# The 48 left-over gated features as 32 and 16 rows in four row groups of TensorE, instead of 48 rows in two

## The chip, the cores and the metric

The kernel runs on one core of one Trainium2 chip. The metric is the device time of one execution in microseconds (us). The engines have short names in the profile: PE is TensorE (PEld its weight loads), DVE is VectorE, ACT is ScalarE, POOL is GpSimd, SP is SyncE; SPq, ACTq and POOLq stand for what their sequencers do, DMA issues above all.

## The reference

`x` is 2048 tokens by 512 features. It is normalised, and two blocks of work are added to it.

```python
def _A_ref(x, wqkv, wo):                  # sliding local attention, 32 heads of 16
    ...
    logits = jnp.einsum('bhsd,bhswd->bhsw', q, kg) * scale     # 8 keys at distance 0, 2, ... 14
    attn = _softmax(logits, axis=-1)
    o = jnp.einsum('bhsw,bhswd->bhsd', attn, vg)
    return (lambda x, *d: x.transpose(*d))(o, 0, 2, 1, 3).reshape(B, S, D) @ wo
def _B_ref(x, w_in, w_sp, b_sp, w_out):   # gated mixer, Fh = 688
    z = _gelu(jnp.einsum('bsd,df->bsf', x, w_in))
    z1 = z[..., :Fh].copy()
    z2 = _layernorm(z[..., Fh:], axis=-1)
    g = jnp.einsum('ts,bsf->btf', w_sp, z2) + b_sp[None, :, None]
    return jnp.einsum('bsf,fd->bsd', z1 * g, w_out)
...
return x + _A_ref(xn, A_wqkv, A_wo) + _B_ref(xn, B_w_in, B_w_sp, B_b_sp, B_w_out)
```

The last step is what the change touches: for every token, a sum over 512 attention features and 688 gated features. 688 is five times 128 and 48 more.

## The kernel before, in words

The tokens are 16 tiles of 128, in two halves `th` of eight tiles. Two hand-written lists, `ten` (TensorE and ScalarE) and `vec` (VectorE), give the order of the work; `advance` interleaves them, so that each engine and each DMA queue gets its instructions in a fixed order. The stages are: layer norm and turning of `x`; the projections; the local attention on VectorE (lines 289 to 360); 16 mixing tiles `M0` to `M15` on TensorE (`mix_tile`, line 374), each with an eviction on ScalarE (line 377) that gives a gate `g`; and the output stage, lines 409 to 431 and 540 to 577.

**Gates and their turning.** `gate(j, g)` (line 382) multiplies tile `j`'s 688 features by its gate on VectorE, and SP then turns the result by DMA transposes into `uT[th]`: six blocks `m` of 128 features, features along the partitions, tokens along the free axis. Of the sixth block (`MF` = 5) 48 rows are features. For the tiles with `j // 2` even one transpose of six blocks does it (line 386), and the 48 rows land on partitions 0 to 47. For the others there are two, one of five blocks (line 388) and one of a block that begins 64 features earlier (line 389), so that the 48 rows land on partitions 64 to 111.

**The output stage.** For each tile of tokens one PSUM bank gathers three products: `gated_full` (line 413), five matmuls of 128 rows by 512 columns; `gated_rest` (line 419), one matmul of 48 rows in a row group of 64 (`tile_position=(r, 0)`, `r` 0 or 64), so that two tiles of tokens can run in TensorE side by side; and the attention, 16 matmuls of 32 rows in one of four row groups (lines 425 and 562), so that four tiles run side by side. Four tiles are a group: tiles 0, 2, 4, 6, then 1, 3, 5, 7, then 8, 10, 12, 14, then 9, 11, 13, 15. `Q0` (`out_pair`) does the first two groups in the order full, rest, rest, attention, attention, full; `Q2` (`out_group`) the third as full, rest, attention; `Q3` (`out_last`) the fourth as attention, rest, full, its last tile in two halves of 256 columns. `finish` and `finish_pair` (lines 430, 437) add `x` on VectorE and send the sum out from SP's queue.

**Loads that the steps touch.** `W0` to `W7` are SP's DMA transposes of the mixing weights (line 367). `load_wout` (lines 401, 403) loads the output weights from ACT's queue, the 48 rows twice, at partitions 0 and 64. `load_wo` (line 398) and the first half of `x` for `finish` (`X0`, line 406) are issued on ACT too, the second half (`X1`, line 406) on SP, into a buffer that `M13` frees. In `vec`, `X1` stands behind `g15`.

Of the kernel before, what the change touches and what calls it, by code (L numbers as in the profile page):

```python
# [7 lines left out]
BF16 = mybir.dt.bfloat16  # L8
# [5 lines left out]
P = 128  # L14
S = 2048
D = 512
# [8 lines left out]
HS = S // 2  # L25
GS = HS // 4
FH = 688
F = 2 * FH
FHALF = FH // 2
MF = FH // P  # L30
FREST = FH - MF * P
# [7 lines left out]
def kernel(  # L39
# [14 lines left out]
    A = nc.scalar  # L54
    G = nc.gpsimd
    PE = nc.tensor
    SP = nc.sync
# [4 lines left out]
    sb = ctx.enter_context(tc.tile_pool(name="sb", bufs=1))  # L62
# [30 lines left out]
    wout = wts[:, DH * D:(DH + MF + 1) * D].rearrange("p (m n) -> p m n", m=MF + 1)  # L93
    qk_r = [sb.tile([P, QKH], BF16, name=f"qk{t}") for t in range(2)]
    qk = [r[:].rearrange("p (a c s) -> p a c s", a=2, c=C) for r in qk_r]
    uT = [r[:, 0:(MF + 1) * HS].rearrange("p (m s) -> p m s", m=MF + 1) for r in qk_r]
    gs = [qk_r[0][:, (MF + 1) * HS + n * FH:(MF + 1) * HS + (n + 1) * FH] for n in range(3)]
    prod = [sb.tile([P, 2 * C * HS], BF16, name=f"prod{n}")[:] for n in range(2)]
    z2_r = sb.tile([P, NT * FH], BF16, name="z2")
# [281 lines left out]
    def gate(j, g):  # L381
        V.tensor_tensor(z1u[:, j, 0:FH], g, z1u[:, j, 0:FH], ALU.mult)
        th, t0 = j // 8, (j % 8) * P

        if j // 2 % 2 == 0:
            SP.dma_start_transpose(uT[th][:, :, t0:t0 + P], z1u[:, j, :])
        else:
            SP.dma_start_transpose(uT[th][:, 0:MF, t0:t0 + P], z1u[:, j, 0:MF * P])
            SP.dma_start_transpose(uT[th][:, MF, t0:t0 + P], z1u[:, j, MF * P - 64:MF * P + 64])

    def idle(n, k=1):

# [6 lines left out]

    def load_wout():  # L400
        A.dma_start(wout[:, 0:MF, :], B_w_out[0:MF * P, :].rearrange("(m p) n -> p m n", p=P))
        for r in (0, 64):
            A.dma_start(wout[r:r + FREST, MF, :], B_w_out[MF * P:FH, :])

    def load_res(th):
        (SP if th else A).dma_start(xr[th], x2[th * HS:(th + 1) * HS, :].rearrange("(i p) d -> p i d", p=P))
# [5 lines left out]
        for m in range(MF):  # L412
            PE.matmul(po[:, cols], uT[th][:, m, t0:t0 + P], wout[:, m, cols], start=(start and m == 0), stop=(stop and m == MF - 1))  # L413

    def gated_rest(tiles, start, stop, bank=None, cols=slice(0, D)):
        for i in tiles:
            r, t0 = 64 * (i // 2 % 2), (i % 8) * P
            b = po[i] if bank is None else bank
            PE.matmul(b[:, cols], uT[i // 8][r:r + FREST, MF, t0:t0 + P], wout[r:r + FREST, MF, cols],  # L419
                      start=start, stop=stop, tile_position=(r, 0))  # L420

    def attention_out(th, s, pos, start, stop):
        for d in range(DH):
# [21 lines left out]
    for i in range(5, NT):  # L445
# [4 lines left out]
        p01 p02 zs8 m10 zn8 zn9 zn10 zn11 p03 W1 f10 zs12 p10 zn12 zn13 zn14 zn15  # L450
        m11 d11 x0 m12 g0 d12 p11 u0 g1 m13 p12 W2 W3 f13 p13 c0 g2
        a0.0 a0.1 g3 x1 a0.2 a0.3 g4 a0.4 g5 a0.5 a0.6 a0.7 g6 u1 a0.8 g7 a0.9 g8 a0.10 g9 a0.11 c1 g10
        a1.0 a1.1 g11 a1.2 a1.3 g12 a1.4 g13 a1.5 g14 a1.6 a1.7 g15 X1 a1.8 a1.9 F0 a1.10 a1.11 F1 F2
    """.split()
    ten = """
        T0 T1 B GL z0 z1 h0 T3 h1 z2 h2 z3 h3 LZ k00 k01 q0 k02 q1 k03 q2 z4 q3 h4 k10 k12 k11 k13
# [75 lines left out]
    def out_pair():  # L532

        first, second = groups[0], groups[1]
        for i in first:
            gated_full(i, po[i], True, False)
        gated_rest(first, False, False)
        gated_rest(second, True, False)
        attention_out(0, 0, [po[i] for i in first], False, True)
        attention_out(0, 1, [po[i] for i in second], False, False)  # L540
        for i in second:
            gated_full(i, po[i], False, True)

    def out_group(n):
        tiles = groups[n]
        for i in tiles:
            gated_full(i, po[i], True, False)
        gated_rest(tiles, False, False)
        attention_out(n // 2, n % 2, [po[i] for i in tiles], False, True)

    def out_last(n):

        tiles = groups[n]
        th, s, last = n // 2, n % 2, tiles[-1]
        hb = [po[last], po[groups[n - 1][0]]]
        cols = [slice(0, D // 2), slice(D // 2, D)]
        for d in range(DH):
            for g in range(4):
                a = slice(32 * g, 32 * g + 32)
                for dd, b, c in [(d, po[tiles[g]], slice(0, D))] if g < 3 else \  # L560
                        [(2 * d % DH + x, hb[d // 8], cols[d // 8]) for x in range(2)]:
                    PE.matmul(b[:, c], op[a, th, dd, s * P:(s + 1) * P], wo_r[a, dd, c],  # L562
                              start=(dd == 0), stop=False, tile_position=(32 * g, 0))
        gated_rest(tiles[:3], False, False)
        for b, c in zip(hb, cols):
            gated_rest([last], False, False, b, c)
        for i in tiles[:3]:
            gated_full(i, po[i], False, True)
            finish(i, po[i])
        for b, c in zip(hb, cols):  # L570
            gated_full(last, b, False, True, c)
            finish(last, b, c)
# [4 lines left out]
    def do(n):  # L577
        k, a = n[0], n[1:]
        i = int(a) if a.isdigit() else 0
        th, w2 = (int(a[0]), int(a[1])) if len(a) == 2 and a.isdigit() else (i, 0)  # L580
        if k == "T":
            turn_pe(i)
            if i == 0:
                idle(1)
        elif n[:2] == "zs":
            z2_stats(int(n[2:]), 4)
        elif n[:2] == "zn":
            z2_norm(int(n[2:]), False)
        elif n == "z0":

            gates["z0"], gates["z1"] = nxt("mm", mm), nxt("mm", mm)
            for t, hh in ((0, 0), (1, 0), (0, 1)):
                z_half(t, 1, gates[f"z{t}"], hh)
        elif n == "z1":
            turn_pe(2)
            z_half(1, 1, gates["z1"], 1)
        elif k == "z":
            gates[n] = z_part(i, 1)
        elif k == "h":
            z2_gelu(i, gates[f"z{i}"])  # L600
        elif k == "q":
            z2_square(i)
        elif k == "k":
            qk_chunks(th, w2 // 2, w2 % 2)
        elif k == "v":
            v_pair(i)
        elif k == "H":
            v_halo()
        elif k == "S":
            head_sum(th, w2)  # L610
        elif k == "B":

            pb = mm[2][:, 1, :].bitcast(BF16)[:, 0:NT]
            PE.transpose(pb, b16[:], ident[0:NT, 0:NT])
            A.copy(b_col[:], pb)
        elif k == "y":
            z1_tile(i)
        elif k == "M":
            gates[i] = mix_tile(i)
        elif k == "W":  # L620
            load_wsp(i)
        elif k == "O":
            load_wo(i) if i < 4 else load_wout()
        elif k == "X":
            load_res(i)
        elif n == "GL":
            A.preload_act_table(ACT.Gelu_apprx_tanh)
        elif n[:2] == "EG":
            A.preload_act_table(ACT.Gelu_apprx_tanh)
        elif n[:2] == "EL":  # L630
            A.preload_act_table_set("natural_log_exp_and_others")
        elif k == "Q":
            [out_pair, None, lambda: out_group(2), lambda: out_last(3)][i]()
        elif k == "F":
            tiles = groups[i]
            for t in (0, 2):
                if (i, t) in ((0, 0), (0, 2), (1, 0)):
                    finish_pair(tiles[t])
                else:
                    finish(tiles[t], po[tiles[t]])  # L640
                    finish(tiles[t + 1], po[tiles[t + 1]])
        elif k == "e":
            softmax_exp(i)
        elif k == "i":
            softmax_inv(i)
        elif k == "s":
            ln_stats(i)
        elif k == "R":
            ln_root_act(i, 1)
        elif k == "V":  # L650
            ln_inv(i)
        elif n == "LE":
            load_early()
        elif k == "r":
            ln_root(i, 1)
        elif k == "n":
            ln_norm(i)
        elif k == "t":
            turn_dma(i)
        elif n == "LZ":  # L660
            load_x(12, 4, A)
        elif n == "LX":
            load_tokens()
        elif n == "LW":
            load_weights()
        elif k == "m":
            run(prod_ops(th, w2)[0])
        elif k == "j":
            run(prod_ops(th, w2)[1])
        elif k == "f":  # L670
            prod_ops(th, w2)[2]()
        elif k == "p":
            prod_ops(th, w2)[3]()
        elif k == "d":
            fold_dma(th, w2)
        elif k == "K":
            k_halo()
        elif k == "x":
            run(softmax_max(i))
        elif k == "u":  # L680
            run(softmax_sum(i))
        elif k == "c":
            run(softmax_scale(i))
        elif k == "g":
            gate(i, gates[i])
        elif k == "a":
            at[int(a[0])][int(a[2:])]()
        done.add(n)
# [53 lines left out]
```

## Time and profile before

| what | value |
|---|---|
| time, median of 3 runs (lowest to highest) | 202.16 us (202.12 to 202.41) |
| the profiled execution's own time | 202.3 us |
| its span in the profile | 200.6 us |
| granted TensorE clock | 0.997 |
| DVE busy | 175.7 us (88%) |
| ACT busy | 96.0 us (48%) |
| POOL busy | 38.7 us (19%) |
| read from HBM, written to it | 10.03 MB, 2.10 MB |

The span runs from the first to the last thing that the profiler saw; the execution's own time is 1.7 us longer. Busy shares are averages over stages. A busy PE means that some matmul is in the array; whether matmuls follow each other at full pace is read from their start times in the timeline, which is in order of time: start, duration, engine, line, operation, tiles, shape, count. Rows of the timeline with a count merge instructions that follow each other; the duration is then that of all of them.

### The profile page before, as it was taken

How to read it: one execution, taken by the hardware profiler on the slowest of the kernel's cores; microseconds unless marked ns; L12 is line 12 of the kernel's file. 1: busy time of each engine (PE TensorE's matmuls, PEld its weight loads, DVE VectorE, ACT ScalarE, POOL GpSimd, SP SyncE). 2: the span in 40 equal slices, each digit the busy share in tenths (PEclk: the TensorE clock that was granted, in tenths of full speed). 3: DMA queues.
4: the chain of work that ended last, by engine and by line, in shares of the span. 5: the costliest groups of instructions: out<-in, count | busy, mean ns of one | idle time of the engine just before them, and what ended most of it. 6: DMA issues, size and time to landing. Idle time of an engine off the chain costs nothing.

```text
span 200.6 us, 3841 instructions
## 1 busy us (share of the span) xinstructions
PE 195.9 (98%) x1587; PEld 118.2 (59%) x1587; DVE 175.7 (88%) x192; ACT 96.0 (48%) x149; POOL 38.7 (19%) x62
## 2 busy tenths in 40 slices
PE   7999999999999999999999999999999999999993
PEld 2645555555656666666566666666666654444652
DVE  4887879999899799999979999999999799897333
ACT  3869879998998647885533264311222110000000
POOL 4366681138660431600000000000000000000000
PEclk9999999999999999999999999999999999999998
DMA  6999459399653837999979099996949611712023
GB/s 183 288 250 197 102 117 303 106 184 206 132 110 29 184 65 146 186 101 89 248 168 192 9 259 281 156 259 128 266 82 272 135 43 39 252 65 105 5 103 105
DMA packets 64289, 30.84 MB, mean 154 GB/s; under 512 B 53440, under 2 KB 62512, under 8 KB 64144
## 3 DMA queue, kind: packets, MB, share of 16 engines
q1 hardware_dynamic: 59296, 19.23, 46.4%
q0 software_dynamic: 1904, 6.59, 16.5%
q10 hardware_dynamic: 3072, 4.78, 8.8%
q8 instruction: 12, 0.20, 0.4%
q14 instruction: 5, 0.04, 0.1%
HBM read 10.03 MB, written 2.10 MB: 60 GB/s over the span
## 4 chain that ended last, share of the span: by engine, by line
PE 88%; DMA 6%; DVE 3%; POOL 1%; issue 0%
PE mm L374 37%; PE mm L209 16%; PE mm L254 10%; PE mm L269 7%; PE mm L413 7%; PE mm L425 5%; DMA z<-in_A_x_dram 4%; DMA xnT<-z 2%; PE aux L413 2%; DVE stats L182 1%; PE mm L562 1%; PE mm L419 1%; PE aux L305 1%; DVE z L196 1%; POOL rstd L187 1%; PE aux L562 0%
## 5 line engine op out<-in xcount | busy, mean ns | idle before, releaser
L374 PE MATMUL mm<-z,wsp 128*128 128x344 bf16 x512 | 75.7, 309 | 0.0
L374 PEld LDWEIGHTS <-wsp 128*128 128x128 bf16 x512 | 50.0, 98 | 24.9 <-issue 0.4
L209 PE MATMUL mm<-wts,xnT 128*128 128x344 bf16 x256 | 40.5, 309 | 0.0
L377 ACT ACTIVATE qk<-mm,b_col 128x688 bf16<-128x688 f32 x16 | 13.3, 834 | 49.8 <-PE mm L374 49.8
L347 DVE TENSOR_TENSOR prod<-vp,a_sb 128x4096 bf16<-128x4096 bf16 x16 | 36.0, 2284 | 0.0
L209 PEld LDWEIGHTS <-xnT 128*128 128x128 bf16 x256 | 24.6, 98 | 14.0 <-issue 0.8
L254 PE MATMUL mm<-xnT,wts 128*128 128x512 bf16 x128 | 29.1, 379 | 0.3 <-DMA xnT<-z 0.2
L289 DVE TENSOR_TENSOR prod<-qk 128x4096 bf16<-128x4096 bf16 (+1 forms) x14 | 27.1, 1979 | 0.1
L351 DVE TENSOR_TENSOR prod<-prod,prod 128x8192 bf16<-128x8192 bf16 x6 | 26.5, 4420 | 0.1
L254 PEld LDWEIGHTS <-wts 128*128 128x128 bf16 x128 | 14.3, 114 | 13.1 <-issue 0.9
L256 ACT CAST qk<-mm 128x1024 bf16<-128x1024 f32 x16 | 16.2, 1011 | 4.8 <-PE mm L254 3.0
L413 PE MATMUL mm<-wts,qk 128*128 128x512 bf16 (+1 forms) x65 | 14.7, 371 | 0.0
L269 PE MATMUL mm<-xnT,wts 128*32 128x512 bf16 x256 | 14.6, 381 | 0.0
L246 ACT ACTIVATE z<-mm 128x688 bf16<-128x688 f32 x16 | 11.8, 745 | 4.5 <-PE mm L209 4.5
L182 DVE BATCH_NORM_STATS2 stats<-z 128x6 f32<-128x512 bf16 x16 | 10.9, 683 | 3.4 <-DMA z<-in_A_x_dram 3.4
L413 PEld LDWEIGHTS <-qk 128*128 128x128 bf16 x85 | 8.1, 98 | 9.2 <-issue 0.6
L220 ACT ACTIVATE z<-mm 128x688 bf16<-128x688 f32 x16 | 11.9, 744 | 1.8 <-PE mm L209 1.8
L225 ACT ACTIVATE z_junk<-z 128x688 bf16<-128x688 bf16 x16 | 12.4, 778 | 0.3
L269 PEld LDWEIGHTS <-wts 128*32 128x32 bf16 x256 | 9.3, 139 | 4.6 <-issue 0.6
L430 DVE TENSOR_TENSOR z<-mm,wsp 128x512 bf16<-128x512 f32 (+1 forms) x8 | 5.0, 653 | 8.0 <-PE mm L425 4.8
L298 POOL DMA_DIRECT2D prod<-prod x8 | 7.1, 933 | 20.9 <-DVE prod L289 19.5
L425 PE MATMUL mm<-wts,xnT 32*128 32x512 bf16 x160 | 10.7, 375 | 0.0
(93 smaller groups left out, 186.2 us busy)
## 6 DMA issues: line engine op xcount, KB each, us to landing
prod<-prod POOLq DMA_DIRECT2D x8, 512.0 KB, 5.7
wts<-in_A_wo_dram ACTq DMA_DIRECT2D x4, 512.0 KB, 5.5
out_dram<-z SPq DMA_DIRECT2D x9, 128.0 KB, 1.7
z<-in_A_x_dram SPq DMA_DIRECT2D x4, 256.0 KB, 4.4
wts<-in_A_wqkv_dram SPq DMA_DIRECT2D x2, 512.0 KB, 7.0
z<-z POOLq DMA_DIRECT2D x2, 512.0 KB, 5.6
wsp<-in_A_x_dram ACTq DMA_DIRECT2D x1, 1024.0 KB, 6.3
wsp<-in_A_x_dram SPq DMA_DIRECT2D x1, 1024.0 KB, 5.3
```

Of the source, the lines that this page charges most:

```text
L182: V.bn_stats(stats[:, i, :], xs[:, i, :])
L209: PE.matmul(pz[:, hh, 0:FHALF], xnT[:, kc, i * P:(i + 1) * P], w_z2[:, hh, kc] if part else w_z1[:, kc, hh * FHALF:(hh + 1) * FHALF], star ...
L254: PE.matmul(pq[:, cc, :], w_c[:, kc], xnT[:, kc, t0:t0 + D], start=(kc == 0), stop=(kc == C - 1))
L256: A.copy(qk[b // 2][:, a, 2 * c2:2 * c2 + 2, o:o + D], pq[:])
L269: PE.matmul(pv[32 * g:32 * g + 32, dd, :], w, r, start=(kc == 0), stop=(kc == C - 1), tile_position=(0, 32 * g))
L289: ops.append(lambda ww=ww, k=k, c=c: V.tensor_tensor(pr[:, ww, c], q[:, c], k[:, c], ALU.mult))
L347: return lambda: V.tensor_tensor(dst, vp[:, :, th, off:off + GS], a_sb[:, th, w].unsqueeze(1).broadcast_to([P, DH, GS]), ALU.mult)
L351: return lambda: V.tensor_tensor(dst, dst, x, ALU.add)
L374: PE.matmul(pg[:, hh, 0:FHALF], w[:, k, (j % 2) * P:(j % 2 + 1) * P], z2[:, k, hh * FHALF:(hh + 1) * FHALF], start=(k == 0), stop=(k == NT ...
L377: A.activation(g.rearrange("p (a b) -> p a b", a=2), pg[:, :, 0:FHALF], ACT.Identity, bias=b_col[:, j:j + 1])
L413: PE.matmul(po[:, cols], uT[th][:, m, t0:t0 + P], wout[:, m, cols], start=(start and m == 0), stop=(stop and m == MF - 1))
L425: PE.matmul(pos[g], op[32 * g:32 * g + 32, th, d, s * P:(s + 1) * P], wo_r[32 * g:32 * g + 32, d, :], start=(start and d == 0), stop=(stop ...
```

## The change

Each tile's 48 left-over features are cut into a part `x = 0` of 32 rows and a part `x = 1` of 16 rows. Tile `i` uses the row group `g` that its attention uses (`i % 8 // 2`). Every gated tile is turned by one six-block transpose, so that the 48 rows always land on partitions 0 to 47, and small SBUF-to-SBUF copies (`spread_rest`) bring the parts to the partitions of their row groups, two tiles (256 tokens) at a time. Of the eight pairs of `g` and `x`, two are in place already, so that there are six copies for each half of the tokens: those of the first half on POOL's queue behind `g7`, those of the second half on SP's queue behind `g9`, `g11`, `g13` and `g15`. Copied parts that would collide in `uT` go to a new strip `uB` in the spent query and key buffer of the second half, and their weights to a new tile `wB`. `load_wout` has eight DMAs instead of three, five on ACT and three on POOL. `X1` moves from behind `g15` to behind `g13`.

```diff
+    uB = [qk_r[1][:, (MF + 1 + n) * HS:(MF + 2 + n) * HS] for n in range(2)]
+    wB = sb.tile([P, D], BF16, name="wB")
...
     def gate(j, g):
         V.tensor_tensor(z1u[:, j, 0:FH], g, z1u[:, j, 0:FH], ALU.mult)
         th, t0 = j // 8, (j % 8) * P
-        if j // 2 % 2 == 0:
-            SP.dma_start_transpose(uT[th][:, :, t0:t0 + P], z1u[:, j, :])
-        else:
-            SP.dma_start_transpose(uT[th][:, 0:MF, t0:t0 + P], z1u[:, j, 0:MF * P])
-            SP.dma_start_transpose(uT[th][:, MF, t0:t0 + P], z1u[:, j, MF * P - 64:MF * P + 64])
+        SP.dma_start_transpose(uT[th][:, :, t0:t0 + P], z1u[:, j, :])
...
-        for r in (0, 64):
-            A.dma_start(wout[r:r + FREST, MF, :], B_w_out[MF * P:FH, :])
+        last, first = B_w_out[MF * P + 32:FH, :], B_w_out[MF * P:MF * P + 32, :]
+        A.dma_start(wout[0:FREST, MF, :], B_w_out[MF * P:FH, :])
+        A.dma_start(wout[64:96, MF, :], first)
+        G.dma_start(wout[96:P, MF, :], first)
+        G.dma_start(wB[32:64, :], first)
+        for r, q in ((0, G), (64, A), (96, A)):
+            q.dma_start(wB[r:r + FREST - 32, :], last)
...
-    def gated_rest(tiles, start, stop, bank=None, cols=slice(0, D)):
-        for i in tiles:
-            r, t0 = 64 * (i // 2 % 2), (i % 8) * P
-            b = po[i] if bank is None else bank
-            PE.matmul(b[:, cols], uT[i // 8][r:r + FREST, MF, t0:t0 + P], wout[r:r + FREST, MF, cols],
-                      start=start, stop=stop, tile_position=(r, 0))
+    def rest_of(i, x):
+        g, t0 = i % 8 // 2, i % 8 * P
+        rows = slice(32 * g, 32 * g + (FREST - 32 if x else 32))
+        if (x == 0) != (g == 1):
+            return rows, uT[i // 8][rows, MF, t0:t0 + P], wout[rows, MF]
+        return rows, uB[i // 8][rows, t0:t0 + P], wB[rows]
+    def gated_rest(tiles, start, last=None):
+        for x in range(2):
+            for i in tiles:
+                rows, u, w = rest_of(i, x)
+                for b, c in last if last and i == tiles[3] else [(po[i], slice(0, D))]:
+                    PE.matmul(b[:, c], u, w[:, c], start=(start and x == 0), stop=False, tile_position=(rows.start, 0))
+    def spread_rest(th, g):
+        t = slice(2 * g * P, 2 * (g + 1) * P)
+        for x in range(2):
+            dst = (uT[th][:, MF] if (x == 0) != (g == 1) else uB[th])
+            n, r = (FREST - 32, 32) if x else (32, 0)
+            if (g, x) not in ((0, 0), (1, 1)):
+                (SP if th else G).dma_start(dst[32 * g:32 * g + n, t], uT[th][r:r + n, MF, t])
...
-        a1.0 a1.1 g11 a1.2 a1.3 g12 a1.4 g13 a1.5 g14 a1.6 a1.7 g15 X1 a1.8 a1.9 F0 a1.10 a1.11 F1 F2
+        a1.0 a1.1 g11 a1.2 a1.3 g12 a1.4 g13 X1 a1.5 g14 a1.6 g15 a1.7 a1.8 a1.9 F0 a1.10 a1.11 F1 F2
...
-        gated_rest(tiles[:3], False, False)
-        for b, c in zip(hb, cols):
-            gated_rest([last], False, False, b, c)
+        gated_rest(tiles, False, list(zip(hb, cols)))
...
         elif k == "g":
             gate(i, gates[i])
+            if i in (7, 9, 11, 13, 15):
+                for g in range(4) if i == 7 else [(i - 9) // 2]:
+                    spread_rest(i // 8, g)
```

In `vec`, `g15` also moves ahead of `a1.7`, an addition over 128x8192 elements of the attention on VectorE (line 351).

More of the change, by code (lines that the diff above doesn't have):

```diff
@@ L536, in out_pair @@
             gated_full(i, po[i], True, False)
-        gated_rest(first, False, False)
-        gated_rest(second, True, False)
+        gated_rest(first, False)
+        gated_rest(second, True)
         attention_out(0, 0, [po[i] for i in first], False, True)
@@ L547, in out_group @@
             gated_full(i, po[i], True, False)
-        gated_rest(tiles, False, False)
+        gated_rest(tiles, False)
         attention_out(n // 2, n % 2, [po[i] for i in tiles], False, True)
```

## The prediction

> **What bounds the kernel now.** I read the page's busy rows first, then the chain that ended last, then the waits of PE, then the timeline of PE in the output stage.
>
> ```profile
> PE 195.9 (98%) x1587; PEld 118.2 (59%) x1587; DVE 175.7 (88%) x192; ACT 96.0 (48%) x149; POOL 38.7 (19%) x62
> ...
> PE   7999999999999999999999999999999999999993
> ...
> PE 88%; DMA 6%; DVE 3%; POOL 1%; issue 0%
> ```
>
> PE is in work in every slice but the first and the last, and 88% of the chain is its own. In the list of waits, PE's matmuls waited for something else for 1.3 us in the whole run, all of it before the output stage. So a nanosecond that leaves PE's stream after `M15` leaves the time, as long as nothing else becomes late, and a faster DMA or VectorE gains nothing by itself.
>
> Is PE at full pace there? In the timeline of PE around `Q0`:
>
> ```profile
> 163.62 4.48 PE L413 MATMUL mm<-wts,qk 128*128 128x512 bf16 x20
> 168.03 0.82 PE L419 MATMUL mm<-wts,qk 48*128 48x512 bf16 x5
> 168.47 0.38 PE L419 MATMUL aux<-wts,qk 48*128 48x512 bf16 x1
> 168.69 0.38 PE L419 MATMUL mm<-wts,qk 48*128 48x512 bf16 x1
> 168.69 0.38 PE L419 MATMUL aux<-wts,qk 48*128 48x512 bf16 x1
> 169.00 0.61 PE L425 MATMUL mm<-wts,xnT 32*128 32x512 bf16 x8
> ```
>
> One matmul lasts 0.379 us, but the next starts sooner: 20 full ones take 4.48 = 19 steps + 0.379, a step of 0.216. The 48-row matmuls go in pairs: eight of them fill four steps (starts at 168.03, .25, .47, .69). The attention goes in fours: 31 steps lie between its first start (169.00) and its last (175.70, in the same timeline), 0.216 each. And at every change of form there is a hole. 163.62 + 20 x 0.216 = 167.94, and the 48-row matmuls start at 168.03: 0.09. 168.03 + 4 x 0.216 = 168.89, and the attention starts at 169.00: 0.11. Attention back to full: 175.92 against 176.01, 0.09.
>
> The same in `Q2` and `Q3`:
>
> ```profile
> 184.75 0.61 PE L419 MATMUL mm<-wts,qk 48*128 48x512 bf16 x4
> 185.29 0.61 PE L425 MATMUL mm<-wts,xnT 32*128 32x512 bf16 x8
> ```
> ```profile
> 192.00 0.42 PE L562 MATMUL mm<-wts,xnT 32*128 32x512 bf16 x3
> 192.35 0.39 PE L419 MATMUL mm<-wts,qk 48*128 48x512 bf16 x1
> ...
> 192.69 0.27 PE L419 MATMUL mm<-wts,qk 48*128 48x256 bf16 x1
> 192.89 0.60 PE L413 MATMUL mm<-wts,qk 128*128 128x512 bf16 x2
> ```
>
> `Q2`: 184.75 + 0.43 = 185.18 against 185.29, a hole of 0.11. `Q3`: 192.22 against 192.35, 0.13; the 48-row part lasts 0.45 (its last half starts at 192.69 and streams 0.11), then 0.09. From 185.29 to 188.76 and on into `Q3`'s attention, also in fours, there is none: it is the change of the number of row groups that costs, not the change of stage.
>
> **The change, part by part.**
>
> *The matmuls.* 17 matmuls of 48 rows become 34 of 32 or 16 rows. They run four abreast in the attention's own row groups, so the steps stay: eight tiles in `Q0` were four pairs and are four fours, in `Q2` two and two, in `Q3` 0.45 becomes 2 x 0.216 = 0.43. Gone are the holes between rest and attention: 0.11 (`Q0`), 0.11 (`Q2`), 0.13 plus 0.02 (`Q3`). Sum -0.37 us. Two holes become full to four groups, which the trace does not show. Bounds: nothing, or the widest hole, 0.13, for each; I take 0.09, that of full to two groups, the nearest row. With the bounds the gain is 0.29 to 0.55.
>
> A rule that speaks against it: the Trainium skill (TensorE: Matmul & The Clock Gate, section "Measured speedup vs the span model") gives 3.07 times for four row tiles of 32 by 512, not four times. This trace shows four matmuls in a step of 0.216; what the rule would make here is the second rival below.
>
> *Transposes.* Eight pairs of DMA transposes on SP become single ones. An issue holds SP's sequencer for 1.2 us (median of lines 386, 388, 389), so 10 us of queue go. Nothing waited for them, so nothing is gained; `W7`, which stood behind `g6`'s second one, is issued about 1.3 us sooner.
>
> *Copies on SP.* Six copies, each set behind the landing of the transposes before it, and what is behind them in the queue waits too: `g10` to `g15`, `X1`, the stores. With 4.5 us from issue to landing (median of line 386) and 0.5 us per copy (line 406's issue), I walk the queue: `g9` issued 145.4, landed 149.9; `g11` issued 151.7, landed 156.2; `g13` issued 158.0, landed 162.5; `X1` 163.5, `g15` 165.3, landed 169.8; its two copies on their way by 170.8, landed by 175.5 with the 4.7 us of the 48-row loads (line 403). `Q2`'s rest needs them at 184.65. Cover: 9 us; cost nothing. The 1 MB of `X1` now moves beside `g14`'s and `g15`'s transposes; it landed in 5.3 us, less than the cover. The first store, at 173.98, is not held up.
>
> *Copies and loads on POOL.* Three loads and six copies. POOL has no work after 85 us. The last two copies wait for `g7` (issued about 141 us); at 1.7 us an issue and 12.4 us to land, the dearest rows of POOL's queue (line 274), they are there by 161, and the rest needs them at 168.03. Cost nothing. DVE beside POOL's issues kept its pace (line 289: 2281 to 2293 ns), so I charge DVE nothing.
>
> *ACT's queue.* Two more issues of 0.5 us (line 403) ahead of the exponential at 119.96. It ends at 122.9 instead of 121.9; DVE reads it at 124.81, and `M7`'s eviction comes at 126.48. A `wo` load behind it now waits for `W5`, issued at 113.6 and landed at 123.9 by the slowest of line 367 (10.3 us): a hold of under 1 us. Cost nothing; PE has three banks in turn.
>
> *`g15` ahead of `a1.7`.* This is the part with the thinnest cover. The timeline of DVE:
>
> ```profile
> 160.45 2.29 DVE L347 TENSOR_TENSOR prod<-vp,a_sb 128x4096 bf16<-128x4096 bf16 x1
> 162.77 4.43 DVE L351 TENSOR_TENSOR prod<-prod,prod 128x8192 bf16<-128x8192 bf16 x1
> 167.11 0.51 DVE L382 TENSOR_TENSOR z<-qk,z 128x688 bf16<-128x688 bf16 x1
> 167.54 4.49 DVE L347 TENSOR_TENSOR prod<-vp,a_sb 128x4096 bf16<-128x4096 bf16 x2
> ```
>
> Now DVE's queue stops at `g15` until `M15` is evicted (163.82 + 0.83 = 164.65, ACT's timeline), 1.9 us idle, with `a1.7` to `a1.11`, `F0` and `F1` behind it. Then 0.43 + 4.34 + 4.49 to 173.95; the 0.64 us that DVE waited for `Q0` before is used up; `F0` 2.40, `a1.10` and `a1.11` 6.66: done at 183.0 instead of 181.7. `Q2`'s attention needs it at 185.08. Cover 2.1 us (3.5 before); cost nothing. `F1` ends at 185.5, `Q3` needs its banks at 188.55; `F0` ends at 176.4, `Q2` needs its banks at 180.34.
>
> *Sum.* 202.30 (the profiled execution: span 200.6 and 1.7 around it) - 0.37 = 201.93. The median of the runs is 0.14 lower than that execution, so the forecast for a median is **201.8 us**, 0.18% less.
>
> **The rivals.**
>
> 1. *SP's copies come late* (the slower end). Mechanism: four landings in a row, each holding the queue. The point is `Q2`'s rest at 184.65. If each landing took the longest of line 386, 9.4 us, `g15` would land at 189.4, its copies at 194.1, and PE would wait 9.5 us: 211. It decides only if the four together are 9 us over the median; each us beyond costs one. For it: the landings range from 2.3 to 9.4. Against: the median is 4.5, and the DMA engines are busy for a third of 160 to 180 us. Chance 5%.
> 2. *Four row groups do not pack fully in so short a run.* If only two ran abreast, as with 64 rows, the eight steps (four in `Q0`, two each in `Q2` and `Q3`) would be sixteen: 8 x 0.216 = 1.7 more, 203.5, slower. Against: after the hole at 169.00 the eight attention matmuls go in fours from the first, 0.61 = 0.216 + 0.379 and little more. 3%. By the skill's factor it would be eight steps times 4 / 3.07 - 1, an estimate of 0.52 more: 202.3, within the bound.
> 3. *The change doesn't do what it says:* going from 32 to 16 rows, or back, opens a hole of its own. Four passes to `x = 1` and three back, 0.1 each, take back 0.7: 202.5, no change by the bound. Against: both parts are set to row groups of 32, and 48 rows in groups of 64 ran pair after pair with no hole. 6%.
> 4. *DVE late at `Q2`*, by over the 2.1 us of cover: 1 us over gives 202.8. 3%.
>
> **How the numbers follow.** The forecast has 81%; 2% are left for what I do not see. About 0.2%, 0.40 us, is what a measurement can tell from no change, so the line lies at 201.76, 0.04 below the forecast; the runs shown scatter by 0.15 about their middle. With the bounds of 0.29 to 0.55, 43 of the 81 lie beyond the line: faster 0.43. Within it lie the other 38, rival 3 and half of the unseen: 0.45. Slower are rivals 1, 2 and 4 and the other half: 0.12. The range: a gain of 0.55 and some scatter give 201.4 below, rival 3 gives 202.5 above; rivals 1, 2 and 4 and the unseen, 13%, stay outside.
>
> **What would show it.** In the changed timeline of PE the rest and the attention follow each other with no hole in `Q0`, `Q2` and `Q3`; the rest starts every 0.216 us in fours; one hole of about 0.09 stands ahead of the rest in `Q0` and `Q2`, none in `Q3`. DVE waits about 1.9 us ahead of `g15` and is through `a1.11` near 183. PE's list of waits shows no DMA and no DVE after `M15`. A hole ahead of the rest of `Q2` with a DMA as releaser is rival 1, ahead of its attention with DVE rival 4, a step over 0.216 within a rest rival 2, a hole between its halves rival 3.

## The result, and the profile after

The changed kernel takes 201.63 us (median of 7 runs, 201.42 to 201.79) against 202.12 us of the kernel before beside it (7 runs). The ratio is 0.9973, 95% interval 0.9962 to 0.9984: 0.3 to 0.8 us faster. Run again later (`e9_change_again`), it gave 0.9985 (0.9968 to 1.0002), an interval that just includes no change. Its profiled execution took 201.5 us with a span of 199.8.

The engines' busy row of the page is nearly as it was; PE still bounds the kernel:

```profile
PE 194.8 (98%) x1604; PEld 119.0 (60%) x1604; DVE 176.0 (88%) x192; ACT 95.9 (48%) x149; POOL 41.1 (21%) x71
```

PE has 17 matmuls more and is busy 1.1 us less; that sum is no measure of the gain, as the kernel before, run again, shows 194.3 (`e1_before_again`, where 8 of the 1587 matmuls have no record). The timeline of PE around `Q0` (start, duration, line, tiles, shape, count; full matmuls are now line 417, the rest 432, the attention 445 and 582):

```profile
163.22 4.48 PE L417 MATMUL mm<-wts,qk 128*128 128x512 bf16 x20
167.63 0.39 PE L432 MATMUL mm<-wts,qk 32*128 32x512 bf16 x1
...
167.86 0.38 PE L432 MATMUL mm<-wB,qk 16*128 16x512 bf16 x1
...
168.08 0.37 PE L432 MATMUL mm<-wts,qk 32*128 32x512 bf16 x1
...
168.30 0.37 PE L432 MATMUL mm<-wB,qk 16*128 16x512 bf16 x1
...
168.51 1.03 PE L445 MATMUL mm<-wts,xnT 32*128 32x512 bf16 x16
```

Four fours start at 167.63, .86, 168.08 and .30, the attention at 168.51: no hole between rest and attention, none between 32 and 16 rows. The hole ahead of the rest is 0.09 (163.22 + 20 x 0.216 = 167.54). From the rest to the attention it took 0.97 us before and takes 0.88 now. `Q2` (0.54 before, 0.45 now) and `Q3`:

```profile
184.26 0.39 PE L432 MATMUL mm<-wts,qk 32*128 32x512 bf16 x1
...
184.71 1.46 PE L445 MATMUL mm<-wts,xnT 32*128 32x512 bf16 x24
```
```profile
191.62 0.37 PE L432 MATMUL mm<-wts,qk 32*128 32x512 bf16 x1
...
191.66 0.27 PE L432 MATMUL aux<-wts,qk 32*128 32x256 bf16 x1
191.77 0.27 PE L432 MATMUL mm<-wts,qk 32*128 32x256 bf16 x1
...
191.88 0.27 PE L432 MATMUL aux<-wB,qk 16*128 16x256 bf16 x1
192.00 0.27 PE L432 MATMUL mm<-wB,qk 16*128 16x256 bf16 x1
192.19 1.25 PE L417 MATMUL mm<-wts,qk 128*128 128x512 bf16 x5
```

In `Q3` the last tile's half-matmuls are the slow strand: they start 0.04 behind the others and follow each other in 0.11 to 0.12, so that the rest takes 0.57 to the full matmuls (0.54 before), while `Q2`'s attention and `Q3`'s, with the hole behind them, shrank from 7.06 (185.29 to 192.35) to 6.91 (184.71 to 191.62). In all: 0.09 + 0.09 + 0.15 - 0.03 = 0.30 us less. From the first rest of `Q0` to the last addition on VectorE it was 29.40 us (168.03 to 197.43) and is 29.11 (167.63 to 196.74):

```profile
197.43 0.42 DVE L430 TENSOR_TENSOR z<-mm,wsp 128x256 bf16<-128x256 f32 x1
```
```profile
196.74 0.42 DVE L450 TENSOR_TENSOR z<-mm,wsp 128x256 bf16<-128x256 f32 x1
```

The first line is of before, the second of the changed kernel. This length, "the stage" below, is the same to 0.01 us in every trace of kernels with the same PE order, which makes it a finer measure than the time.

Two things are left over. The first rest starts 0.40 earlier (167.63 against 168.03), and behind the last store's landing the span ends sooner: 0.91 us against 1.03.

### The profile page after: what moved, and what is told of

Read it like the earlier page. It is cut to its first block, busy times and chain, and to the rows that moved or that the text cites. A ratio compares the mean times of both kernels' runs of the same rounds, so it can differ in the third digit from the quotient of the medians.

```text
span 199.8 us, 3885 instructions
## 1 busy us (share of the span) xinstructions
PE 194.8 (98%) x1604; PEld 119.0 (60%) x1604; DVE 176.0 (88%) x192; ACT 95.9 (48%) x149; POOL 41.1 (21%) x71
## 4 chain that ended last, share of the span: by engine, by line
PE 95%; DMA 1%; DVE 1%; SPq 0%; issue 0%
PE mm L378 37%; PE mm L213 19%; PE mm L258 14%; PE mm L273 7%; PE mm L417 7%; PE mm L445 5%; PE aux L417 2%; DMA z<-in_A_x_dram 1%; PE mm L582 1%; PE mm L432 1%; PE aux L309 1%; PE aux L205 0%; PE aux L582 0%; DVE z L200 0%; DVE stats L186 0%; DVE z L450 0%
## 5 line engine op out<-in xcount | busy, mean ns | idle before, releaser
L440 POOL DMA_DIRECT2D qk<-qk x6 | 3.0, 500 | 50.5 <-DMA wB<-in_B_w_out_dram 27.9
L386 DVE TENSOR_TENSOR z<-qk,z 128x688 bf16<-128x688 bf16 x16 | 8.2, 510 | 4.3 <-ACT qk L381 4.3
```

## The experiments

Each kernel was timed in three or five rounds against the kernel before on the same chip. "End" is from the landing of the last store (by the trace, 2.12 to 2.15 us after the last addition starts) to the end of the span. The last column but one is worked out from the trace: 1 + (stage + end - 29.40 - 1.03) / 202.

```
kernel                    first rest  stage   end   worked out  ratio to before (95%)
before                      168.03    29.40  1.03   1           -
changed                     167.63    29.11  0.91   0.9980      0.9973 (0.9962 to 0.9984)
e1_before_again             167.72    29.40  1.03   1.0000      1.0008 (0.9999 to 1.0018)
e2_wB_alone                 167.61    29.41  1.29   1.0013      1.0010 (1.0001 to 1.0019)
e3_order_alone              167.97    29.40  1.04   1.0000      1.0006 (0.9990 to 1.0022)
e4_no_copies                167.85    29.11  1.28   0.9998      0.9994 (0.9986 to 1.0003)
e5_turns_alone              167.46    29.40  1.30   1.0013      1.0014 (1.0004 to 1.0024)
e6_two_more_holes           167.74    29.32  0.91   0.9990      0.9987 (0.9977 to 0.9998)
e7_vector_late              167.71    31.64  0.92   1.0105      1.0152 (1.0125 to 1.0178)
e8_old_order                168.19    29.10  0.91   0.9979      0.9989 (0.9973 to 1.0005)
e9_change_again             167.46    29.10  0.91   0.9979      0.9985 (0.9968 to 1.0002)
e10_last_tile_first         168.16    29.11  0.92   0.9980      0.9981 (0.9965 to 0.9997)
e11_vector_late_by_half     167.66    29.51  0.91   1.0000      1.0003 (0.9983 to 1.0023)
e12_one_more_dma            167.57    29.11  1.35   1.0001      0.9995 (0.9984 to 1.0006)
```

### Is the early start part of the change?

`e1_before_again` is the kernel before, without an edit.

> The kernel before, unchanged, run once more against itself. Theory A (the gain is the holes of the output stage, 0.30 us from the first full matmul of Q0 on; the 0.40 us by which that stage began earlier in the changed kernel's trace, 163.22 against 163.62, is how the loads of x happened to land): ratio 1.000 with an interval of about 0.001 to each side, and the start of Q0 in this trace lies anywhere between 163.2 and 163.7, while the stage itself, first full matmul of Q0 to last half-matmul of Q3, again takes 33.07. Theory B (the early 0.40 belongs to the change: layout of SBUF or the new loads): Q0 starts at 163.6 again.

`e2_wB_alone`:

```diff
+    wB = sb.tile([P, D], BF16, name="wB")
...
+        G.dma_start(wB[32:64, :], first)
+        for r, q in ((0, G), (64, A), (96, A)):
+            q.dma_start(wB[r:r + FREST - 32, :], last)
```

> The kernel before with the tile wB and its four loads added (every later tile moves by 1 KB), and nothing that reads them. Theory A: no effect, ratio 0.999 to 1.001, output stage 33.07. Theory B: Q0 starts at about 163.2 and the ratio is 0.998 (0.4 us of 202).

The same program started its first rest at 168.03 and at 167.72. Over the table the old rest starts between 167.46 and 168.03 (mean 167.76), the changed one between 167.46 and 168.19 (mean 167.77). So the 0.40 is not the change. In the trace of before a tile of `x` kept VectorE waiting for 0.59 us ahead of 13.83 and PE stood at 20.20; in `e1` and in the changed kernel's trace neither shows. The traces of `e3`, `e8` and `e10` have this wait too, with 0.52 to 1.02 us, and these and before are the four with the latest start, whichever rest they have. (`e6` waits for 0.59 us as well and starts at 167.74, so the wait is not the whole of it.) `wB` does nothing to the stage. Theory B falls.

### Do the order, the transposes or the copies matter?

`e3_order_alone`, the kernel before with:

```diff
-        a1.0 a1.1 g11 a1.2 a1.3 g12 a1.4 g13 a1.5 g14 a1.6 a1.7 g15 X1 a1.8 a1.9 F0 a1.10 a1.11 F1 F2
+        a1.0 a1.1 g11 a1.2 a1.3 g12 a1.4 g13 X1 a1.5 g14 a1.6 g15 a1.7 a1.8 a1.9 F0 a1.10 a1.11 F1 F2
```

> The kernel before with the changed order only: X1 behind g13, g15 ahead of a1.7. Theory A: no effect on the time, ratio 0.999 to 1.001, stage 33.07; VectorE is idle about 1.9 us ahead of g15 and is through a1.11 about 1 us later than before (182.9 against 181.7). Theory C (the order brings part of the gain): ratio 0.998 or less, or a stage shorter than 33.0.

`e8_old_order`, the changed kernel with those two lines the other way round:

> The changed kernel with the old order of VectorE's list: g15 behind a1.7, X1 behind g15. Theory A: the order is worth nothing either way; from the first rest of Q0 to the last addition on VectorE 29.10 us, ratio to before 0.998 to 1.000, though SP sends the last copies some 2 us later. Theory F (without the new order the last copies come late): PE waits for a DMA ahead of Q2's rest and the stage is longer than 29.2.

`e5_turns_alone`, the kernel before with single transposes, as in the change, and whole 48-row copies:

```diff
...
+            if i in (7, 11, 15):
+                for g in (1, 3) if i == 7 else [(i - 9) // 2]:
+                    t = slice(2 * g * P, 2 * (g + 1) * P)
+                    u = uT[i // 8]
+                    (SP if i > 7 else G).dma_start(u[64:64 + FREST, MF, t], u[0:FREST, MF, t])
```

> One six-block transpose for every tile, as in the change, but the 48 rows stay whole, in two row groups of 64; four copies bring them to partition 64 (two on POOL's queue for the first half of the tokens, two on SP's for the second). Theory A (only the holes count; eight transposes fewer on SP gain nothing): from the first rest of Q0 to the last addition on VectorE 29.40 us, as in all four traces with the old rest (the two with the new one have 29.11), and a ratio to before of 0.9995 to 1.002, as the kernel before run against itself gave. Theory D (transposes fewer are part of the gain): 0.998 or less.

`e4_no_copies`, the changed kernel without the calls of `spread_rest` (so it leaves out what brings six of the eight parts to their places):

> The changed kernel without its twelve small copies, so that six of the eight parts of the left-over features are read from stale rows. Theory A (copies are wholly hidden): the same time as the changed kernel, ratio to before 0.997 to 0.9985, stage 32.77 as in the changed kernel. Theory D (the copies cost something on PE or DVE): faster than the changed kernel, ratio under 0.996, or a stage under 32.7.

All four keep the stage of their matmul order, 29.40 or 29.10: order, transposes and copies are hidden. One thing came out the other way than expected: in `e8_old_order` SP sent the last two copies not later but sooner, at 170.37 against 173.09, since there `X1` stands behind them in its queue. The first line is of the changed kernel, the second of `e8_old_order`:

```profile
173.09 1.18 SPq L440 DMA_DIRECT2D qk<-qk  x2
```
```profile
170.37 1.15 SPq L440 DMA_DIRECT2D qk<-qk  x2
```

And by its median `e4_no_copies` was not as fast as the changed kernel (0.9994; the interval overlaps that of `e9`), and `e5_turns_alone` was slower than before, though their stages are right. What they have in common with `e2_wB_alone` is the end, 1.28 to 1.30 instead of 0.91 or 1.03; that is taken up below.

### Is it the holes?

`e6_two_more_holes`, the changed kernel with, in `out_pair` (the new last argument marks the end of the sum in PSUM):

```diff
-        gated_rest(second, True)
         attention_out(0, 0, [po[i] for i in first], False, True)
-        attention_out(0, 1, [po[i] for i in second], False, False)
+        attention_out(0, 1, [po[i] for i in second], True, False)
         for i in second:
-            gated_full(i, po[i], False, True)
+            gated_full(i, po[i], False, False)
+        gated_rest(second, False, None, True)
```

> The changed kernel with the rest of the second group (tiles 1, 3, 5, 7) moved behind that group's full matmuls, so that PE passes once more from full rows to four row groups and back; no matmul more or less. Theory A: two holes of 0.09 more, stage 29.11 + 0.18 = 29.29 us, ratio about 0.0009 above that of the changed kernel run beside it. Theory E (the holes are not what the change saved; it is the matmuls in fours that are faster): stage 29.11.

Its timeline of PE, where the two forms now meet:

```profile
178.45 1.24 PE L417 MATMUL aux<-wts,qk 128*128 128x512 bf16 x5
179.62 0.39 PE L432 MATMUL mm<-wts,qk 32*128 32x512 bf16 x1
...
180.17 0.39 PE L417 MATMUL mm<-wts,qk 128*128 128x512 bf16 x1
```

178.45 + 5 x 0.216 = 179.53: a hole of 0.09 ahead; 179.62 + 2 x 0.22 = 180.06: 0.11 behind. The stage grew by 0.21 with no matmul more. A hole costs what the prediction took for it. Theory E falls, also by the timelines: the steps of `Q0`'s rest are 0.22 us in pairs (168.03, .25, .47, .69 before) and 0.22 in fours (167.63, .86, 168.08, .30 now), so that a step of fours is no shorter.

`e10_last_tile_first`, the changed kernel with:

```diff
-            for i in tiles:
+            for i in tiles[3:] + tiles[:3] if last else tiles:
...
-            for g in range(4):
+            for g in (3, 0, 1, 2):
```

> The changed kernel with the last tile of Q3, the one in two halves, issued ahead of the other three in the attention and in the rest of Q3. In the changed kernel the rest of Q3 takes 0.57 us to the first full matmul instead of 0.43 + 0.09, because the halves start 0.04 behind the others and follow each other in 0.113 instead of 0.108. If the late start comes from the order of issue, the stage is 29.06 us instead of 29.10; if it comes from the halves themselves, 29.10 again. The time cannot tell either: ratio to before 0.998 to 1.000.

The stage stayed at 29.11, and the halves started 0.04 to 0.05 behind the others and 0.11 apart, as in the changed kernel: the order of issue is not why `Q3`'s rest is slow. That the halves themselves are is the reading left; a rest without halves was not tried.

### How much cover has VectorE?

`e7_vector_late` and `e11_vector_late_by_half`, the changed kernel with one of these ahead of `a1.10`:

```diff
+            V.tensor_tensor(t[1], t[1], t[1], ALU.max)
```
```diff
+            V.tensor_tensor(t[1][:, 0], t[1][:, 0], t[1][:, 0], ALU.max)
```

> The changed kernel with one needless operation on VectorE, the largest of 128x8192 with itself (no value changes), ahead of the addition a1.10: some 4.4 us. In the changed kernel's trace a1.11 ended at 182.64 and Q2's attention began at 184.71: cover 2.07. If that cover is right, PE waits 4.4 - 2.07 = 2.3 us ahead of Q2's attention and the time is 2.3 us above the changed kernel's, ratio to it 1.0115. If the order with g15 ahead of a1.7 already cost time, the whole 4.4 appears (1.022); if there is more slack than I see, less than 2.

> The changed kernel with a needless operation on VectorE of half the size (128x4096, some 2.2 us) ahead of a1.10. With a cover of 2.07, PE waits 0.1 to 0.2 us ahead of Q2's attention, the stage is 29.2 to 29.3 and the time 0.15 us above the changed kernel's; without the long gap of the other run the granted clock stays near 1.0 in every execution. If the cover is under 1.5, the time is 0.7 us or more above.

The lines of `a1.11` on VectorE and of the attention behind it on PE, from `e7_vector_late`, with the next line of VectorE, which starts when `a1.11` is through:

```profile
184.97 2.29 DVE L368 TENSOR_TENSOR xnT<-prod 128x4096 bf16<-128x4096 bf16 x1
187.18 0.68 DVE L461 TENSOR_TENSOR z<-mm,wsp 128x512 bf16<-128x512 f32 x1
```
```profile
187.32 2.98 PE L449 MATMUL mm<-wts,xnT 32*128 32x512 bf16 x52 [2.36 <-DVE xnT L368]
```

PE starts 0.14 after VectorE is through (0.13 in `e11_vector_late_by_half`: 185.00 and 185.13), so the cover was 1.93, not 2.07, and the stages grew by 2.54 and 0.40, somewhat over the 2.3 and 0.2 expected. Rival 4's point is real, and the change stays 1.9 us away from it. That the time of `e7_vector_late` rose by more than its stage is told in the last section.

### What is the rest of the gain?

`e9_change_again` is the changed kernel without an edit.

> The changed kernel, unchanged, once more, beside the three others and on one chip with them. Theory A: the stage is 29.11 again and the median 0.3 us (0.15%) below that of kernels with the old rest run in the same way; against the runs of the kernel before the ratio is 0.998 to 1.000, nearer to 1 than the 0.9973 first measured. Theory B (0.2 us or more of the gain lie ahead of the output stage and belong to the change): 0.9973 again, and Q0's rest starts at 167.6 again.

`e12_one_more_dma`, the changed kernel with:

```diff
+    pad = sb.tile([16, 256], BF16, name="pad")
...
             load_res(i)
+            if i:
+                SP.dma_start(pad[:], B_w_out[0:16, 0:256])
```

> The changed kernel with one more load of 8 KB on SP behind X1 that nothing reads. Each DMA on SP or ACT takes the next of eight completion semaphores in turn, and at the end SP waits for the eight one after the other, 0.06 us each, in a fixed order. In the kernel before and in the changed one the last store has the one that is waited for last; the extra load moves it to one that is waited for second. Theory G (these waits are on the path): from the landing of the last store to the end of the span 0.92 + 6 x 0.06 = 1.29 us, as in the kernels wB_alone, turns_alone and no_copies (1.28 or 1.29), the stage unchanged at 29.10, and the ratio to before near 0.9998 instead of 0.9985. Theory H (those three had another reason): 0.92, ratio 0.998 to 0.999.

SP's list of waits, changed kernel, then `e12_one_more_dma` (line 758 or 761 is the end of the program; total, times, longest):

```profile
SPq L758 <- DMA out_dram<-z: 0.7, 2, 0.4
```
```profile
SPq L761 <- DMA out_dram<-z: 1.1, 1, 1.1
```

In the first, SP checks seven semaphores while the stores are still on their way and meets the last landing at its last wait. In the second it stands at the second wait until the last store lands, and then does the other seven, 0.06 us each. The expectation had counted six, hence 1.35 instead of 1.29. Theory G holds and H falls by the end in the trace; the ratio's interval would allow both.

Which semaphore the last store gets can be counted. In the traces SP and ACT take the eight in turn, and together they issue 80 DMAs in before and in the changed kernel, 82 in `e2`, 74 in `e4` and in `e5`, 81 in `e12`. 80 is ten full rounds, so that the last store has the last semaphore. 82 and 74 leave two over, 81 leaves one, and so the last store has the second or the first of the eight there. The changed kernel has eight transposes fewer, six copies and two loads more on these queues: that this comes to 80 again is luck.

So the changed kernel's end differs from that of before by less, 0.12 us. Between POOL's last two steps before the final barrier lie 0.16 us in the traces of before, `e1` and `e3`, and 0.04 in all others. In these three the last step of ACT, a `DRAIN`, comes late and takes long: it starts 0.67 us after the last landing (0.39 in the changed kernel), and POOL goes on 0.03 us after its end. The first line is of before, the second of the changed kernel (count; shortest, median and longest in ns; first and last start; the last step is the shortest of its two):

```profile
L737 ACTq DRAIN  x2: 141/502/864, 163.8 to 200.2; - x2
```
```profile
L758 ACTq DRAIN  x2: 14/439/864, 163.4 to 199.3; - x2
```

Why ACT's step is late there, no run shows. No step of the change set out to save these 0.12 us.

## Why the prediction was right, and where it was off

The forecast was 201.8 us, 0.37 us less; the stage (0.30) and the end (0.12) together give 0.41 before rounding, and the measured ratio stands for 0.3 to 0.8. The holes are what was forecast. That the sum comes so near to 0.37 is partly luck: the holes gave less, and the end, for which the prediction has no term, made up for it.

- **PE bounds the kernel:** right. PE's matmuls waited for 1.8 us in the changed kernel, all in the first 10 us.
- **The holes:** right in mechanism. The hole from full rows to four row groups, which had to be bounded, is 0.09, the value taken. The size was off: 0.30 instead of 0.37. The term that was mis-sized is the steps: a four of the rest takes 0.22, not 0.216 (0.02 more in `Q0` and in `Q2`), and `Q3`'s rest 0.57 with its hole instead of 0.52; the hole ahead of `Q3`'s rest was worth 0.15 and not 0.13.
- **Four abreast:** the sixteen matmuls of `Q0`'s rest take 0.88 us, 0.055 each against 0.216 for one, 3.9 times. The 3.07 of the Trainium skill (TensorE: Matmul & The Clock Gate, "Measured speedup vs the span model") isn't borne out in this trace, and rivals 2 and 3 fall with these lines: a step of 0.22 is over 0.216, the sign given for rival 2, but by 0.004 and not by double, and nothing opens between 32 and 16 rows.
- **Transposes and copies cost nothing:** right, by `e4` and `e5`. The walk of SP's queue held to the third of the four sets of copies (162.5 forecast, 161.68 in the trace). The last set went at 173.09 and 173.7 instead of by 170.8: the load of `X1`, moved ahead of `g14`'s and `g15`'s transposes, took 8.3 us to land instead of 5.3, and these transposes landed only at 172.5 and 173.0. With `X1` behind the copies (`e8`) they went at 170.37. The copies landed by 176.7, and the rest wanted them at 184.26. On POOL the last two copies went at 147.4 and 147.9, and the prediction had them landed by 161. On ACT the exponential began 0.8 us later than before (120.74 against 119.96; 1.0 forecast), and PE's list of waits shows none for it.
- **`g15` ahead of `a1.7`:** VectorE stood 1.95 us (1.9 forecast) and was through `a1.11` 1.3 us later in the stage:

```profile
164.29 0.52 DVE L386 TENSOR_TENSOR z<-qk,z 128x688 bf16<-128x688 bf16 x1 [1.95 <-ACT qk L381]
164.72 4.42 DVE L355 TENSOR_TENSOR prod<-prod,prod 128x8192 bf16<-128x8192 bf16 x1
...
182.64 0.68 DVE L457 TENSOR_TENSOR z<-mm,wsp 128x512 bf16<-128x512 f32 x1
```

  Hidden, as forecast, and by `e8` not needed either.
- **What was missed:** the end. The prediction has no term for the 3 us behind the start of the last addition. They differ by up to 0.4 us between kernels with the same stage, as much as the whole gain forecast. With one DMA more on SP the change would have shown almost nothing, as `e12` did.

## What to carry to other kernels

Where TensorE is never idle, look for holes at the changes of form in its start times: multiply the step by the count and compare with the next start. Put work of one row grouping side by side; each change cost 0.09 to 0.15 us here. When a few tenths of a microsecond are at stake, compare a stage in the traces and not the times alone: here the stage repeats to 0.01 us, while the start of the same program varied by 0.3 (168.03 and 167.72). And ask which completion SP will wait for last: one DMA more on SP moved the end by 0.4 us here.

## What the runs showed of the hardware

- **The end of a program.** In all these traces SP waits for the eight completion semaphores of its own and ACT's DMAs in one fixed order, 0.06 us each. With the last store on the last of them the changed kernel's end takes 0.91 us from its landing; on an early one it takes 1.28 to 1.35 (`e4`, `e12`).
- **A change of row grouping.** Between full rows, two and four row groups TensorE's start times show holes of 0.09 to 0.15 us; between 32 and 16 rows in the same four groups there is none.
- **A pause of PE and the clock.** In `e7_vector_late` PE paused for 2.5 us ahead of `Q2`'s attention. Three of its six runs had a mean granted clock of 0.992 and took 205.67 to 205.91 us, the three at 1.0 took 204.12 to 204.94. The two medians, 205.75 and 204.62, lie 1.1 us apart. The profiled execution was one at 1.0, so no trace shows where the clock was lower, and that the pause is the cause is inferred: it is what sets this kernel apart from `e11_vector_late_by_half`, which paused for 0.4 us there and has 0.998 or more in all ten runs. The Trainium skill (TensorE: Matmul & The Clock Gate, "Why this matters for your kernels") warns of pauses over about 3 us; if the pause is the cause, 2.5 us was enough in half of the runs.
